# A gated linear recurrence and a feed-forward layer on one core: the last four slabs as one group

## The chip, the cores and the metric

The kernel runs on one core of a Trainium2 chip. The core has five engines that each work through their own list of instructions in order: TensorE (PE, matrix products into PSUM), VectorE (DVE), ScalarE (ACT, functions from tables), GpSimd (POOL) and SyncE (SP, which here only issues transfers). Loads of stationary operands for PE have a row of their own in the profile (PEld). The metric is the device time of one run in microseconds; the kernel before has a median of 265.34 us over 3 runs (265.21 to 265.36). The profiled execution has a span of 263.2 us.

## The reference, cut to what matters

First a recurrence with a complex decay, for 4 batches, 8 heads, 768 steps and 48 features:

```python
mag = np.sqrt(a_re * a_re + a_im * a_im)
scale = np.minimum(mag, 0.999) / (mag + 1e-06)
a_re_n, a_im_n = (a_re * scale, a_im * scale)
for t in range(S):
    new_re = ar * S_re - ai * S_im
    new_im = ar * S_im + ai * S_re
    S_re, S_im = (new_re + kv, new_im)      # kv: outer product of k[t] and v[t]
    y[:, :, t] = np.einsum('bhd,bhde->bhe', q[:, :, t], S_re)
```

Then y, as x of 3072 tokens by 384, goes through a gated feed-forward layer with 1536 inner features:

```python
gate = 1.0 / (1.0 + np.exp(-(x @ w_gate)))
val = x @ w_val
return (gate * val @ w_out).astype(np.float32)
```

## The kernel before, in words

**Slabs.** The 768 steps of a batch are cut into 6 chunks of 128. A chunk of one batch, with all 8 heads, is a *slab*: 128 steps on the partitions by 384 columns. There are 24, numbered chunk by chunk (slab m is batch m % 4 of chunk m // 4). Within a slab the recurrence becomes products of matrices: running sums of the logarithm of the decay and of its angle, q and k scaled by the exponentials and turned by the angles, masked scores of q against k, and a state of 48 by 48 for each head that is carried from chunk to chunk.

**Groups.** Slabs are taken in groups, by SIZES. A group shares the steps on its whole tile of decays (four activations on ScalarE), and, after the recurrence, one feed-forward part: tokens of all its slabs are the columns of its products. With four slabs these are 512 columns, with two 256. Chunk 5, the last, is cut into two groups of two in the kernel before, so there are seven groups.

**Steps.** Every piece of work is a *step* with a short name and a number (slab, or group and block of features). In the order of the data:

- lr, la (L541): loads of a_re and a_im of a slab; sq: squares, on ScalarE (L571) or VectorE (L568); add and min (L577, L584): squared magnitude and its cap.
- lna, lnm (L592, L598), inv (L603), r (L609), atan (L687): logarithms, ratio and angle, for a group.
- cl (L618): running sum of logarithms by a product in fp32; ee (L625, L627): its exponentials; scr, rbe, arr: decay over a chunk, by way of HBM.
- lk, lq, lv (L541): loads of k, q and v; qke (L680): q and k times the exponentials; v16 (L673): v in half precision.
- ct (L701, L704, L723), r16 (L730), nid (L737), hop (L714), cr (L747): running sum of the angle, less whole turns, with the carry from the chunk before; from chunk 2 on the carry is added by a small transfer, hop.
- ab, cs (L758, L769 to L772): cosine and sine; ks, qs (L782): k and q turned, written into a place with six slots.
- transposing of those: by PE (tp, qkT: L820, L821, L827) for the first 13 slabs, by transfers (xk, xq: L803) for the others.
- sc (L839), mst (L847): scores and their mask; u, x16, kv, P (L861, L870, L879, L889): the state; y (L905, L907), y16 (L507): the output of the recurrence; xp, xt (L925, L931): its transposition into xt, the input of the feed-forward part.
- pg and pv (L944): products with w_gate and w_val, for 12 blocks of 128 features, three matmuls each; tanh (L954): the gate, as a tanh; p (L960): (tanh + 1) times the value; po (L980): products with w_out, in three parts of four matmuls for each slab; ot (L507) and st (L998): output and its store.

pg and pv of a group can start once xt of all its slabs is there.

**Order.** Nothing is reordered by a compiler: the order is by hand. TIMES holds a due time for every step, in us; all steps are sorted by it, and each engine gets its instructions in that order. SLOTS says for each buffer of a ring which of its places a tile takes, and WARM how many matmuls on zeros (L1014) are put ahead of a step, into the tile that it will overwrite; they keep PE's clock up while it would wait. When ScalarE needs another set of function tables than the one it holds, a load of a table (L1008) is put in. The due times do not delay anything: an instruction starts when its engine has come to it and its inputs and places are there.

The lines that the change touches are tables alone. SIZES is used in

```python
FIRST = [sum(SIZES[:i]) for i in range(len(SIZES))]
for g, n in enumerate(SIZES):
    m0 = FIRST[g]
    spans = [(i, min(i + PAIR, n)) for i in range(0, n, PAIR)]
nt = n * L
```

and the last slab's output is computed in two halves of 192 columns, so that its first half can be stored while the second is computed.

Of the kernel before, what the change touches and what calls it, by code (L numbers as in the profile page):

```python
# [34 lines left out]
SIZES = [4, 4, 4, 4, 4, 2, 2]  # L35
TIMES = {
    "wg": [
        22.939, 53.604, 46.761],
    "wv": [
        41.489, 57.377, 49.918],  # L40
    "wo": [
        69.384, 65.792, 74.71],
    "lr": [
        0.6, 2.76, 4.68, 1.01, 7.56, 11.4, 21.96, 9.48, 29.035, 36.763,
        34.603, 40.603, 53.574, 65.05, 65.46, 69.488, 91.541, 102.449, 94.661,
        101.489, 129.641, 144.257, 166.92, 169.283],
    "la": [
        1.42, 5.64, 6.6, 3.72, 8.52, 13.32, 21, 14.28, 30.955, 37.723, 44.224,
        38.683, 56.839, 59.355, 66.25, 71.918, 91.951, 100.699, 93.701,
        100.289, 132.576, 136.865, 169.693, 171.783],  # L50
    "sq": [
        5.29, 9.13, 10.09, 7.21, 12.09, 16.953, 26.869, 17.819, 35.119,
        43.141, 51.317, 50.58, 63.932, 71.041, 72.995, 77.727, 96.326, 108.9,
        100.923, 107.686, 141.821, 149.617, 173.785, 176.745],
    "add": [
        6.159, 9.999, 11.044, 8.079, 13.107, 17.97, 27.886, 19.639, 42.886,
        44.046, 52.222, 58.417, 64.837, 72.97, 75.53, 81.618, 99.728, 109.941,
        101.828, 108.978, 146.191, 151.929, 174.69, 177.65],
    "min": [
        10.579, 11.624, 21.17, 29.665, 54.424, 59.948, 80.715, 83.639,  # L60
        111.798, 110.895, 156.229, 185.814],
    "lna": [
        10.958, 34.211, 53.348, 80.235, 115.074, 157.704, 179.252],
    "lnm": [
        12.335, 32.834, 62.547, 84.606, 112.957, 159.31, 186.78],
    "inv": [
        13.712, 36.423, 64.669, 81.743, 117.191, 158.572, 180.12],
    "r": [
        16.087, 15.221, 39.728, 37.968, 67.623, 70.424, 89.8, 94.764, 118.736,
        126.526, 159.477, 181.025],  # L70
    "cl": [
        13.863, 16.67, 20.01, 15.378, 36.319, 37.411, 34.836, 38.883, 64.65,
        68.978, 65.942, 65.296, 86.871, 112.147, 102.388, 106.72, 115.007,
        117.823, 134.023, 131.882, 160.664, 162.183, 192.729, 188.19],
    "ee": [
        15.356, 20.801, 21.541, 20.061, 37.8, 38.54, 35.683, 39.73, 66.046,
        69.825, 68.557, 72.255, 87.718, 114.334, 111.477, 112.217, 116.451,
        118.669, 137.956, 136.74, 161.511, 163.03, 193.576, 189.037],
    "scr": [
        23.34, 22.65, 23.62, 22.37, 44.634, 48.008, 43.366, 48.288, 94.111,  # L80
        85.572, 83.333, 75.858, 96.031, 114.89, 112.033, 112.773, 118.11,
        120.772, 143.977, 139.687, 185.698, 186.798, 194.287, 194.567],
    "rbe": [
        31.915, 61.755, 97.571, 116.08, 149.099, 193.468, 197.428],
    "lk": [
        19.08, 12.36, 23.9, 10.44, 30.542, 22.93, 46.624, 26.99, 86.538,
        74.318, 80.523, 75.448, 103.409, 82.923, 106.289, 108.241, 133.536,
        118.468, 143.567, 127.135, 153.417, 186.388, 158.185, 173.993],
    "lq": [
        20.04, 18.12, 27.942, 16.2, 39.643, 35.803, 47.598, 49.079, 89.103,  # L90
        79.105, 83.883, 76.705, 104.369, 95.621, 107.249, 112.313, 135.905,
        125.596, 148.689, 134.624, 157.07, 193.058, 158.595, 187.724],
    "lv": [
        15.24, 17.16, 35.013, 42.956, 54.152, 67.21, 41.563, 81.87, 92.361,
        85.162, 115.54, 96.581, 105.329, 118.878, 87.987, 130.695, 139.277,
        121.052, 148.279, 126.005, 185.978, 192.648, 170.823, 177.453],
    "v16": [
        20.593, 42.309, 50.738, 49.342, 66.832, 77.757, 59.371, 87.463,
        98.286, 94.188, 124.976, 103.369, 118.084, 149.97, 105.026, 147.632,
        171.078, 133.794, 189.145, 130.048, 191.369, 202.109, 188.569, 183.572],  # L100
    "qke": [
        23.805, 22.502, 32.19, 20.947, 45, 47.581, 55.616, 60.85, 96.525,
        88.039, 91.561, 85.702, 112.701, 115.256, 128.287, 134.657, 148.209,
        164.194, 152.883, 143.564, 162.433, 196.377, 194.498, 198.138],
    "atan": [
        17.39, 41.764, 76.35, 105.833, 131.576, 183.842, 183.105],
    "ct": [
        18.918, 20.953, 26.326, 21.761, 43.292, 45.031, 52.079, 49.241,
        90.692, 86.225, 90.046, 89.232, 122.944, 118.469, 127.422, 128.468,
        141.143, 143.731, 163.053, 166.071, 196.201, 198.47, 197.014, 210.201],  # L110
    "r16": [
        19.765, 22.036, 28.601, 24.671, 44.785, 46.524, 55.711, 53.381,
        92.893, 87.268, 96.023, 92.427, 124.789, 119.316, 128.465, 129.397,
        145.892, 151.604, 163.899, 167.878, 197.481, 201.212, 205.333, 211.683],
    "nid": [
        21.599, 22.636, 29.201, 25.271, 47.8, 47.124, 57.969, 53.981, 95.223,
        89.07, 97.975, 98.138, 125.513, 120.184, 129.686, 131.483, 151.699,
        153.161, 165.483, 170.802, 198.308, 205.144, 206.601, 216.88],
    "cr": [
        25.889, 26.259, 30.065, 26.629, 49.053, 49.423, 59.91, 56.806, 95.586,  # L120
        95.956, 102.136, 104.169, 125.876, 126.246, 130.049, 132.953, 152.062,
        156.041, 176.375, 174.522],
    "cs": [
        23.575, 24.732, 30.542, 29.067, 49.793, 48.055, 58.646, 56.019,
        97.088, 89.752, 102.535, 99.273, 126.617, 120.704, 130.419, 133.335,
        153.726, 154.883, 165.847, 171.166, 198.671, 205.507, 207.141, 217.243],
    "ks": [
        25.137, 27.735, 34.253, 31.008, 53.847, 50.186, 62.767, 63.633,
        100.35, 91.041, 105.9, 103.014, 130.62, 121.993, 133.214, 138.058,
        155.016, 167.012, 173.321, 172.455, 201.678, 209.351, 208.486, 218.665],  # L130
    "qs": [
        26.003, 29.533, 35.985, 36.851, 56.177, 51.783, 69.053, 65.696,
        101.548, 97.554, 107.254, 108.12, 132.348, 123.325, 143.227, 141.296,
        157.143, 168.81, 175.386, 177.145, 203.143, 210.817, 215.684, 219.531],
    "ab": [
        30.542, 29.067, 49.12, 48.055, 58.364, 55.245, 97.088],
    "tp": [
        31.002, 27.003, 30.555, 36.965, 39.976, 38.436, 40.822, 42.338,
        64.204, 60.921, 63.757, 63.31, 71.142, 78.268, 80.861, 67.236,
        111.701, 114.56, 108.014, 104.329, 119.514, 113.24, 112.793, 121.647,  # L140
        155.897, 136.164],
    "qkT": [
        33.056, 33.654, 37.717, 38.315, 42.217, 39.084, 41.618, 43.881,
        65.097, 61.569, 67.856, 64.499, 73.684, 79.317, 83.445, 68.455,
        112.348, 115.942, 110.784, 109.586, 120.713, 114.145, 113.546,
        124.191, 156.545, 146.957],
    "sc": [
        39.752, 39.529, 41.273, 44.584, 47.577, 44.807, 46.784, 48.678,
        69.624, 75.674, 80.638, 79.114, 78.044, 81.308, 86.002, 84.728,
        117.176, 119.961, 115.653, 114.337, 127.199, 125.29, 117.599, 126.326,  # L150
        158.294, 153.974, 148.462, 148.686, 161.31, 159.167, 162.829, 160.041,
        177.84, 180.206, 182.371, 190.582, 191.856, 193.375, 188.836, 189.059,
        217.265, 217.042, 220.489, 220.712, 225.009, 222.435, 227.095, 226.217],
    "mst": [
        40.553, 39.953, 42.815, 45.85, 48.521, 45.251, 47.456, 49.586, 71.295,
        77.073, 81.062, 79.916, 78.711, 81.732, 86.669, 85.212, 117.6,
        121.312, 116.54, 115.343, 127.866, 126.187, 118.666, 126.786, 158.718,
        154.398, 148.887, 151.004, 161.781, 160.25, 163.254, 162.381, 179.769,
        180.968, 186.393, 191.006, 192.589, 193.799, 190.083, 189.483,
        218.066, 217.466, 220.913, 221.978, 227.064, 223.102, 227.663, 229.162],  # L160
    "kv": [
        40.622, 58.131, 77.844, 72.884, 102.188, 82.829, 122.094, 117.399,
        132.528, 134.669, 150.851, 145.025, 166.717, 170.965, 176.345,
        179.358, 201.706, 211.495, 207.411, 220.935],
    "P": [
        41.152, 60.655, 78.245, 74.282, 104.834, 84.746, 122.859, 118.2,
        142.162, 135.07, 153.269, 145.426, 169.676, 178.704, 183.373, 181.567,
        204.867, 213.384, 212.918, 221.512],
    "y": [
        41.739, 46.584, 51.711, 50.533, 78.714, 85.602, 83.678, 88.502,  # L170
# [130 lines left out]
}  # L301
WARM = {
    ('cl', 0): 41,
    ('cl', 2): 8,
    ('cl', 3): 2,
    ('ct', 0): 7,
    ('ct', 2): 16,
# [737 lines left out]
```

## Time and profile before

| | |
|---|---|
| time, median of 3 | 265.34 us |
| span of the profiled execution | 263.2 us |
| PE busy | 240.2 us (91%) |
| VectorE busy | 211.7 us (80%) |
| ScalarE busy | 178.5 us (68%) |
| GpSimd busy | 150.7 us (57%) |
| loads of tables (L1008) | 23, 29.5 us |
| moved by DMA | 38.12 MB, 145 GB/s in the mean |

How to read it: the busy time of PE contains the time in which a matmul drains, so a full row does not say that PE runs at its best pace; the distance between starts of neighbouring matmuls does. In a row of the groups, the numbers behind the bar are the busy time, the mean of one in ns, and the idle time of the engine ahead of them with what ended it. The chain that ended last is followed back from the last instruction, at each step to what released it or to the instruction before it on its engine.

### The profile page before, as it was taken

What the parts mean: (1) busy time and instruction counts of PE and PEld (TensorE: products, weight loads), DVE (VectorE), ACT (ScalarE), POOL (GpSimd) and SP (SyncE); (2) the same over time, 40 slices, a digit from 0 to 9 for tenths busy, and PEclk for the clock granted to TensorE, in tenths of its full rate; (3) what the DMA queues carried; (4) which work ended last, traced back from release to release, by engine and by line L of the source; (5) the groups of instructions that cost most, each with busy time, mean ns of one, the idle gap of its engine ahead of it and who ended that gap; (6) DMA issues with size and microseconds to landing.
All of it is one profiled execution on the core that took longest, in us unless ns stands there. A gap on an engine that the chain in (4) does not pass through costs nothing.

```text
span 263.2 us, 5644 instructions
## 1 busy us (share of the span) xinstructions
PE 240.2 (91%) x2066; PEld 150.2 (57%) x2066; DVE 211.7 (80%) x363; ACT 178.5 (68%) x288; POOL 150.7 (57%) x165
## 2 busy tenths in 40 slices
PE   6076598999999999999999999999999999999995
PEld 6043375454657654547765456654457544679784
DVE  2658998798988979979997889898859689987453
ACT  3799698299999478999469648758974373214240
POOL 3035409969599999679877299833687642010000
PEclk9669989999999999999999999999999999999999
DMA  7999999999999939975699969859964455651011
GB/s 146 218 214 176 192 149 188 205 166 182 139 205 202 181 74 169 176 157 95 121 209 204 151 135 149 194 111 178 221 133 90 66 110 108 73 147 36 8 54 60
DMA packets 174859, 38.12 MB, mean 145 GB/s; under 512 B 167768, under 2 KB 174832, under 8 KB 174832
## 3 DMA queue, kind: packets, MB, share of 16 engines
q1 hardware_dynamic: 170336, 34.20, 68.3%
q0 software_dynamic: 4496, 3.57, 9.7%
q8 instruction: 16, 0.26, 0.4%
q14 instruction: 11, 0.09, 0.1%
HBM read 30.74 MB, written 4.76 MB: 135 GB/s over the span
## 4 chain that ended last, share of the span: by engine, by line
PE 58%; ACT 15%; DMA 8%; DVE 7%; SPq 4%; issue 3%; POOL 3%; ACTq 0%; POOLq 0%
PE o L980 16%; PE v L944 13%; PE g L944 11%; PE cl L618 4%; ACT L1008 4%; DMA a<-in_a_im_dram 3%; PE sc L839 3%; SPq L541 3%; PE ct L723 3%; DMA a<-in_a_re_dram 3%; ACT a L687 2%; POOL qk L680 2%; DMA qk<-in_q_dram 2%; ACT g L954 1%; POOL a L609 1%
## 5 line engine op out<-in xcount | busy, mean ns | idle before, releaser
L954 ACT ACTIVATE g<-g 128x512 f16<-128x512 f32 (+1 forms) x84 | 43.6, 542 | 37.4 <-PE g L944 34.5
L960 DVE SCALAR_TENSOR_TENSOR p<-g,v 128x512 f16<-128x512 f16 (+1 forms) x84 | 49.6, 607 | 20.9 <-ACT g L954 10.1
L944 PE MATMUL v<-xt,wv 128*128 128x512 f16 (+1 forms) x252 | 57.3, 348 | 0.5 <-ACT g L954 0.4
L944 PE MATMUL g<-xt,wg 128*128 128x512 f16 (+1 forms) x252 | 56.9, 348 | 0.5 <-DVE xt L931 0.3
L980 PE MATMUL o<-wo,p 128*128 128x384 f16 (+1 forms) x300 | 54.6, 319 | 0.5 <-ACT g L954 0.5
L577 POOL TENSOR_TENSOR lm<-sq 128x384 f32<-128x384 f32 x20 | 23.2, 1174 | 30.7 <-DVE sq L568 18.9
L680 POOL TENSOR_TENSOR qk<-qk,ee 128x768 f32<-128x768 f32 x20 | 38.2, 1915 | 2.4 <-ACT ee L627 1.6
L847 DVE TENSOR_TENSOR mst<-sc,msk_t 128x512 f16<-128x512 f32 x48 | 32.3, 685 | 4.7 <-PE sc L839 4.6
L944 PEld LDWEIGHTS <-wv 128*128 128x128 f16 x252 | 24.1, 98 | 20.6 <-issue 1.6
L980 PEld LDWEIGHTS <-p 128*128 128x128 f16 x300 | 27.3, 97 | 14.9 <-issue 0.9
L944 PEld LDWEIGHTS <-wg 128*128 128x128 f16 x252 | 23.6, 97 | 20.3 <-issue 2.6
L618 PE MATMUL cl<-lm,wl_t 128*128 128x384 f32 x48 | 22.2, 557 | 9.2 <-ACT lm L598 8.9
L1008 ACT ACT_TABLE_LOAD x23 | 29.5, 1283 | 0.4
L782 DVE TENSOR_TENSOR qst<-qk,cs 128x768 f16<-128x768 f32 x24 | 26.1, 1092 | 0.0
L782 DVE TENSOR_TENSOR kst<-qk,cs 128x768 f16<-128x768 f32 x24 | 24.4, 1029 | 1.4 <-ACT cs L772 0.9
L609 POOL TENSOR_TENSOR a<-a 128x768 f32<-128x768 f32 x10 | 18.1, 1816 | 9.1 <-DMA qk<-in_q_dram 7.8
L571 ACT ACTIVATE sq<-a 128x768 f32<-128x768 f32 x19 | 16.0, 846 | 6.3 <-DMA a<-in_a_im_dram 6.2
L861 POOL TENSOR_TENSOR state<-state,arr 128x384 f32<-128x384 f32 x16 | 13.9, 869 | 11.0 <-DVE state L889 10.7
L827 DVE COPY qkT<-tp 128x1024 f16<-128x1024 f16 x26 | 17.3, 682 | 1.5 <-PE tp L821 1.5
L625 ACT ACTIVATE ee<-cl 128x384 f32<-128x384 f32 x24 | 12.0, 500 | 9.0 <-PE cl L618 6.9
L839 PEld LDWEIGHTS <-qkT 128*128 128x128 f16 x192 | 13.4, 97 | 7.4 <-issue 2.7
L723 PE MATMUL ct<-a,wt_t 128*128 128x384 f32 x40 | 16.9, 507 | 0.6 <-ACT a L687 0.5
(76 smaller groups left out, 428.9 us busy)
## 6 DMA issues: line engine op xcount, KB each, us to landing
a<-in_a_re_dram SPq DMA_DIRECT2D x24, 192.0 KB
a<-in_a_im_dram SPq DMA_DIRECT2D x24, 192.0 KB
qk<-in_k_dram SPq DMA_DIRECT2D x24, 192.0 KB
v<-in_v_dram SPq DMA_DIRECT2D x24, 192.0 KB
qk<-in_q_dram SPq DMA_DIRECT2D x24, 192.0 KB
out_dram<-ot SPq DMA_DIRECT2D x23, 192.0 KB
wg<-in_moe_w_gate_dram POOLq DMA_DIRECT2D x3, 384.0 KB, 6.4
wv<-in_moe_w_val_dram POOLq DMA_DIRECT2D x3, 384.0 KB, 6.4
```

Source lines behind the costliest of these rows:

```text
L577: eng(g).tensor_tensor(out=T[LM][:, s], in0=T[SQ][:, 0], in1=T[SQ][:, 1], op=ALU.add)
L618: nc.tensor.matmul(T[CL][:, :HD], wl_t, T[LM][:, s], start=True, stop=True)
L680: eng(g).tensor_tensor(out=T[QK], in0=T[QK], in1=T[EE], op=ALU.mult)
L723: nc.tensor.matmul(T[CT][:, :HD], wt_t, T[A][:, 1, s], start=True, stop=False, skip_group_check=True)
L782: nc.vector.tensor_tensor(out=T[SL][i].rearrange("p h (r x) -> p h r x", r=2)[:, :, :, 0:D], in0=heads(T[QK][:, i]).unsqueeze(2) .broadcas ...
L839: nc.tensor.matmul(sc[:, i], kt, qt, start=True, stop=True)
L847: nc.vector.tensor_tensor(out=T[MS], in0=T[SC], in1=msk_t.unsqueeze(1).broadcast_to([L, 4, L]), op=ALU.mult)
L944: nc.tensor.matmul(T[ACC][:, :nt], w[:, j, fb * 128:fb * 128 + 128], T[XT][:, j, :nt], start=(j == 0), stop=(j == 2))
L954: nc.scalar.activation(out=T[G16][:, :nt], in_=T[PG][:, :nt], func=FT.Tanh, scale=0.5)
L960: nc.vector.scalar_tensor_tensor(out=T[PT][:, fb, :nt], in0=T[G16][:, :nt], scalar=1.0, op0=ALU.add, in1=T[PV][:, :nt], op1=ALU.mult)
L980: nc.tensor.matmul(T[PO][:, :wd], T[PT][:, fb, s * L:(s + 1) * L], wo16[:, fb, c0:c0 + wd], start=(fb == 0), stop=(fb == NFB - 1))
L1008: nc.scalar.preload_act_table_set(SETS[key[1]])
```

## The change

SIZES gets six groups of four, so that the last four slabs share one feed-forward part of 512 columns, and the steps on a group's tile of decays are done once for the four. It is for fewer and larger instructions on PE, VectorE and ScalarE in the last chunk. As there are fewer steps and their sizes differ, all due times, places in the rings and fillers were computed anew, for all 24 slabs and not for the last four alone. The number of fillers goes from 150 to 211. The code below the tables is unchanged.

```diff
-SIZES = [4, 4, 4, 4, 4, 2, 2]
+SIZES = [4, 4, 4, 4, 4, 4]
 TIMES = {
...
     "lr": [
...
-        129.641, 144.257, 166.92, 169.283],
+        131.683, 136.462, 153.209, 141.067],
     "la": [
...
-        132.576, 136.865, 169.693, 171.783],
+        133.153, 132.373, 157.251, 141.847],
...
     "xt": [
...
-        195.883, 196.5, 197.215, 196.234, 225.6, 225.866, 235.784, 237.901],
+        192.648, 199.472, 198.936, 199.802, 228.285, 229.255, 229.52, 229.786],
     "pg": [
-        55.379, 58.979, 66.588, 57.321, 70.494, 73.731, 67.683, 62.015,
...
+        56.731, 57.378, 74.734, 58.673, 70.649, 68.261, 73.439, 62.637,
...
     "po": [
...
-        239.236, 235.654, 236.958, 238.258, 246.108, 248.069, 249.708,
-        248.719, 249.048, 249.379, 250.358, 250.689, 251.018],
...
+        249.683, 250.993, 246.743, 247.393, 248.703, 251.643, 252.293,
+        252.943, 245.763, 248.043, 248.373, 249.353, 250.333, 250.663],
...
 WARM = {
-    ('cl', 0): 41,
-    ('cl', 2): 8,
-    ('cl', 3): 2,
-    ('ct', 0): 7,
-    ('ct', 2): 16,
-    ('y', 2): 11,
-    ('sc', 3, 1): 9,
+    ('cl', 0): 80,
+    ('cl', 3): 5,
+    ('ct', 0): 10,
+    ('ct', 1): 3,
+    ('ct', 2): 4,
+    ('ct', 3): 6,
+    ('sc', 0, 0): 4,
+    ('y', 0): 3,
+    ('sc', 2, 1): 9,
+    ('y', 2): 2,
+    ('y', 3): 10,
     ('pg', 0, 0): 11,
-    ('cl', 4): 15,
-    ('cl', 6): 30,
+    ('cl', 4): 10,
+    ('cl', 6): 37,
+    ('ct', 4): 5,
+    ('ct', 5): 10,
+    ('ct', 6): 2,
 }
```

## The prediction, made before the changed kernel was run

> **What bounds the kernel now.** I read the page first, for the busy shares and the forty slices.
>
> ```profile
> PE 240.2 (91%) x2066; PEld 150.2 (57%) x2066; DVE 211.7 (80%) x363; ACT 178.5 (68%) x288; POOL 150.7 (57%) x165
> PE   6076598999999999999999999999999999999995
> PEclk9669989999999999999999999999999999999999
> ```
>
> TensorE is full from the ninth slice (about 58 us) to the end, and its clock is low only in the head. Since a busy PE row counts drain time, I checked this against the cadence, in the chain that ended last:
>
> ```profile
> 223.43 0.65 PE v L944 x3
> 224.07 1.30 PE o L980 x8
> 240.22 0.33 PE g L944 x3
> 256.74 3.29 PE o L980 x32
> 260.06 0.36 DVE ot L507
> ```
>
> Three 512-column matmuls take 0.65 us (216 ns each), three 256-column ones 0.33 us (109 ns), four of 384 columns 0.65 us (162 ns). From neighbouring rows, fp32 products over 384 columns come at 325 ns a record, 128-column ones at 55.5 ns and 48-column ones at about 25 ns. Multiplying by the counts by form gives 217.0 us of useful PE work; 21.1 us of it is ordered ahead of the first gate product, 195.9 us behind it. From that product to the last one the trace has 260.06 - 58.65 = 201.4 us. So behind 58.65 us all PE waiting together is only 5.5 us, and the kernel is: **head (58.65) + PE work (195.9) + waits (5.5) + tail (3.1) = 263.2**.
>
> ```profile
> 57.57 0.78 PE L1014 MATMUL g<-zero 128*128 128x128 f16 x11
> 58.65 0.81 PE L944 MATMUL g<-xt,wg 128*128 128x512 f16 x3 [0.29 <-DVE xt L931]
> ```
>
> This timeline of PE shows the head's end: filler matmuls, then the first gate product, released by VectorE's xt.
>
> Each step has its due time in TIMES, so trace minus table is how far the chip lags the plan. The first pg is due at 55.379 and starts at 58.65: lag 3.27. It grows to 3.8 at 91 us, 4.6 at 96, 5.6 at 115, 6.65 at 143, 6.97 at 188, 8.2 at 197, and then stays at 8.3 to 8.5 up to the last product. The table thus orders the work and also spaces PE's work rightly; what it misses is 3.3 us in the head and 5.2 us of small waits between 60 and 200 us. The last of these, 1.25 us, shows in the chain:
>
> ```profile
> 176.08 0.57 SPq L541
> ...
> 176.70 4.67 DMA a<-in_a_im_dram
> ...
> 182.85 1.07 ACT g L954 x2
> ...
> 188.97 1.28 ACT L1008
> ...
> 190.27 0.61 ACT g L954
> ...
> 190.91 2.11 PE o L980 x12
> ```
>
> A load of a_im for slab 22 was due at 169.7, was issued at 176.70, and held back ScalarE's square; the tanh queued behind it was late, and with it p and the output products.
>
> **What the Trainium skill says.** "TensorE: Matmul & The Clock Gate", section "Wait — 56ns, not 53.3ns?", gives a fixed 2.5 ns for each matmul above its columns. This trace agrees: 2 x 109.2 - 216 is 2 to 3 ns, so halving the width is nearly free on PE. The same page, "What's actually happening", has the clock gate halve the clock after an idle window of some 3.4 us; PEclk at 0.58 between 10 and 20 us agrees. "ScalarE: Activation LUTs", section "What ACT_TABLE_LOAD costs", has 1283 ns for each load; the 23 loads here measure 1283 ns.
>
> **The change part by part.** The rows by form that price it:
>
> ```profile
> L944 PE MATMUL v<-xt,wv 128*128 128x256 f16 x72 | 11.0, 272 | 0.0
> L960 DVE SCALAR_TENSOR_TENSOR p<-g,v 128x512 f16<-128x512 f16 x60 | 40.0, 682 | 13.9 <-ACT g L954 6.5 <-PE v L944 6.1 <-ACT sq L571 0.9
> L960 DVE SCALAR_TENSOR_TENSOR p<-g,v 128x256 f16<-128x256 f16 x24 | 9.6, 419 | 7.0 <-ACT g L954 3.6 <-PE v L944 3.0
> L954 ACT ACTIVATE g<-g 128x512 f16<-128x512 f32 x60 | 34.7, 606 | 16.4 <-PE g L944 15.0 <-DVE p L960 1.1
> L954 ACT ACTIVATE g<-g 128x256 f16<-128x256 f32 x24 | 8.9, 384 | 21.0 <-PE g L944 19.6 <-DVE p L960 1.4
> ```
>
> *Merging on PE.* 144 matmuls of 109.2 ns (15.7 us) become 72 of 216 ns (15.55): 0.2 us less on the bound engine. The output products are per slab and stay.
>
> *Merging on VectorE and ScalarE.* p: 24 x 419 = 10.06 us becomes 12 x 682 = 8.18, so 1.9 us less; tanh: 24 x 384 becomes 12 x 606, also 1.9 us less; four steps on slabs (two Ln, Exp, Arctan) go from two of 844 ns to one of about 1488, 0.8 us less. Table loads: reading the new TIMES in order gives 20 in place of 23, 3.8 us less. All this lies beside PE, so I cost it at nothing by itself; it can only shorten the 5.2 us of waits.
>
> *The tail.* Before, the last feed-forward part had 256 tokens and ran while the other half was still being prepared. Now all four slabs must be transposed into xt before the last part begins. The new table puts its first pg at 230.223, and the last xt at 229.786 in place of 237.901, so the recurrence has to finish 8 us sooner. What hides this is other PE work placed ahead of 230: the group before it is ordered up to there. PE gaps planned there are small: from first pg to last po the new table spans 252.943 + 0.65 - 56.731 = 196.9 us for 195.9 us of work, about 0.9 us of planned gaps against none before. After my 0.2 us rounding: **+0.7**.
>
> *The head.* First pg due at 56.731 in place of 55.379, with 20.93 us of useful work ahead of it in place of 21.13. So 1.35 + 0.2 = **+1.55 us**. I see no reason that the head's lag of 3.27 should differ: the same loads come at about the same places (45 of slabs due by 50 us in both tables), and the fillers rise from 150 to 211, each in a planned gap (37 ahead of the fifth cl, in a gap of 3.99 us; at the halved clock's 111 ns that is 4.1).
>
> *The end.* The last output was the second 192 columns of slab 23 (0.36 us of VectorE, 96 KB store). Now slab 22's full 384 columns come last: 0.56 us and 192 KB. 0.2 on VectorE; the extra 96 KB at the span's mean of 145 GB/s would be 0.7, at the 200 GB/s of the busiest slices 0.5, and much of this overlaps issuing; bounds 0 to 0.7, taken as 0.2. **+0.4**.
>
> *Waits.* The late loads of slabs 22 and 23 were due at 166.9 to 171.8 for squares due at 173.8 and 176.7. The new table asks for them at 153.2 and 157.3 for a square at 180.5 (slab 22) and at 141.1 and 141.8 for one at 154.6 (slab 23): 23 and 13 us of room in place of 4 to 5. I expect the 1.25 us of lag that they made to go: **-1.2**. The waits between 60 and 188 us (some 3.7 us) I keep: the order there is as crowded, with 79 loads due by 80 us in place of 77 (a weight load, twice the size, counted as two).
>
> Sum: 1.55 + 0.7 + 0.4 - 1.2 = +1.45, so 265.34 + 1.45 = **266.8 us**.
>
> **The rivals.**
>
> *Waits stay as they were.* If the 1.2 us moves elsewhere rather than goes, 265.34 + 2.65 = 268.0. For it: every freshly made order meets its own late load, SyncE's issues lagging the table by up to 9 us in this trace. Against it: the loads near the end have much room now.
>
> *The last handoff stalls.* VectorE has 28.2 us of work due between 200 and 230 us, and the chain from Arctan (due 192.9) to the last xt runs through one set of four slabs with only 4.0 us from the last transposing load to its score products (4.9 before). If that chain lags PE by two or three us, PE stands before the last part: 268.0 + 2.5, about 270.5. Against it: with 27.5 us due on VectorE in the same stretch before, PE did not wait at all after 205 us.
>
> *Faster, the other side.* The relief of ScalarE (5.7 us with three loads fewer) and VectorE takes most of the mid-kernel waits, which do pass through ScalarE (tanh lags to 5.7 us at 113 us while p lags 4.7). If 4 of the 5.2 us go: 265.34 + 2.65 - 4.0 = 264.0. Against it: the mid waits start at loads and at GpSimd, which the merging doesn't touch before 150 us.
>
> **How the numbers follow.** Forecast (266.8) 0.42, waits stay (268.0) 0.25, last handoff (270.5) 0.11, faster (264.0) 0.22. The head's lag of 3.27 alone may turn out 1 us either way, which spreads each of them. The range leaves out most of the handoff case and the better half of the faster one: 264.4 to 269.4. From the same cases: faster by over 0.2% (below 264.8) 0.19, within 0.2% 0.13, slower 0.68.
>
> **What would show it.** Right: first gate product of full width at 59.5 to 60.5 us, about 196 us of PE work behind it with no long stretch of another engine, the last product ending at 261.5 to 262.5; 20 or 21 table loads; no wait at slabs 22 and 23. Wrong: first gate product by 58.7 us, or its lag not growing between 60 and 200 us (then the faster case); a gap of over 1 us on PE, released by xt, ahead of the last gate products (then the handoff); large idle rows of PE waiting on tanh or p.

## The result and the profile after

The changed kernel takes 267.07 us against 265.27 us (265.01 to 265.36) for the kernel before beside it: ratio 1.0069, 95% interval 1.0049 to 1.0088. It is slower by about 1.8 us, close to the forecast of 266.8. Runs over 1.5% above the fastest of the same kernel (three of the changed kernel's eleven, at 272.2 to 272.3 us, one of e_end and two of e_port) count in the medians but not in the ratios. First the page of the changed kernel: busy times, PE's row of the slices, and two of the groups.

```profile
PE 242.8 (91%) x2055; PEld 147.9 (56%) x2055; DVE 209.9 (79%) x351; ACT 172.9 (65%) x269; POOL 152.0 (57%) x164
PE   8186488887999999999999999999999999999994
...
L958 ACT ACTIVATE g<-g 128x512 f16<-128x512 f32 x72 | 41.7, 598 | 42.6 <-PE g L948 30.3
L964 DVE SCALAR_TENSOR_TENSOR p<-g,v 128x512 f16<-128x512 f16 x72 | 48.0, 683 | 15.6 <-PE v L948 8.4
```

The merging did what it was for: 72 tanh and 72 p in place of 84 each, all of 512 columns, 5.6 us less on ScalarE and 1.8 us less on VectorE. PE's row is full from the eleventh slice on; the slice before it, from 59.7 to 66.3 us, holds the pause that is shown below.

I split each profiled execution at the first gate product of full width and at the end of the last product. The splits sum to the span, so this table says where each kernel's time lies, in us:

| kernel | to the first gate product | from it to the last product's end | from there to the end | span |
|---|---|---|---|---|
| before | 58.65 | 201.37 | 3.15 | 263.17 |
| changed | 60.88 | 200.75 | 3.74 | 265.37 |
| difference | +2.23 | -0.62 | +0.59 | +2.20 |

The profiled execution of the kernel before took 264.89 us, 0.4 less than its median of 265.27; that of the changed kernel took its median. This is why the spans differ by 2.20 us and the medians by 1.80.

So the whole loss is in the head and in the last store; the long stretch of PE between them, where the merging acts, is a little shorter. Trace minus table, the measure of the prediction, divides it further:

| at (us of the trace) | 60 | 70 | 120 | 186 | 200 | 250 |
|---|---|---|---|---|---|---|
| lag before | 3.26 | 3.50 | 5.70 | 6.93 | 8.22 | 8.34 |
| lag changed | 4.14 | 5.55 | 6.11 | 7.54 | 7.63 | 7.85 |

Three things are to be seen. The changed kernel enters with 0.9 us more lag. It loses 1.4 us at once between 60 and 70, where the kernel before loses 0.2. And the step of 1.3 us between 186 and 200 is gone. The list of PE's waits behind the head (columns: us in total, times, longest) has little in it; these are the longest:

```profile
PE ct L741 <- DVE r L734: 1.3, 1, 1.3
PE y L909 <- POOL x L874: 0.4, 1, 0.4
```

The longest of them in the timelines of PE, VectorE and GpSimd (columns: start, duration):

```profile
60.88 1.46 PE L948 MATMUL g<-xt,wg 128*128 128x512 f16 x6
...
65.56 0.32 PE L741 MATMUL ct<-r,nid_t 128*128 128x384 f16 x1 [1.28 <-DVE r L734]
```

```profile
61.61 0.95 DVE L786 TENSOR_TENSOR kst<-qk,cs 128x768 f16<-128x768 f32 x1
62.48 2.56 DVE L786 TENSOR_TENSOR qst<-qk,cs 128x768 f16<-128x768 f32 x1
64.97 0.54 DVE L734 TENSOR_SCALAR r<-ct 128x384 f16<-128x384 f32 x1
```

```profile
62.22 2.01 POOL L613 TENSOR_TENSOR a<-a 128x768 f32<-128x768 f32 x1 [2.08 <-ACT a L607]
```

PE stands 1.28 us for r16, which stood on VectorE behind a qs that took 2.56 us where its twin took 0.95. A GpSimd product had begun 0.26 us before that qs and ended at 64.23; the qs ended at 65.04, 0.81 us later. "SBUF — State Buffer" of the Trainium skill, section "SBUF: two separate sides", says why: a port pair that VectorE, with two inputs in SBUF, and GpSimd take as an exclusive lock for a whole instruction, so that the second one waits. This trace agrees: the held qs needs nearly its normal time after the GpSimd operation, and no more. The kernel before has this too, at 59.44 us:

```profile
59.44 2.02 DVE L782 TENSOR_TENSOR qst<-qk,cs 128x768 f16<-128x768 f32 x1
```

Beside it GpSimd ran qke from 58.83 to 60.64, and this qs ended at 61.46, again 0.82 us after. There PE waited for nothing behind it. Over whole traces the holds are alike: of the products that turn q and k, 10 take over 0.15 us longer than 0.95 us before, 5.1 us in excess together, and 9 after, 4.8 us. What differs is who stood behind one of them.

The end of the changed kernel, in VectorE's timeline, is the 384-column output that the prediction named:

```profile
261.67 0.56 DVE L511 TENSOR_SCALAR ot<-o 128x384 f32<-128x384 f32 x1 [1.12 <-PE o L984]
```

### The profile page after: what moved, and what is told of

It reads as the page before. It is cut to its first block, busy times and chain, and to the rows that moved or that the text cites. A ratio compares the mean times of both kernels' runs of the same rounds, so it can differ in the third digit from the quotient of the medians.

```text
span 265.4 us, 5540 instructions
## 1 busy us (share of the span) xinstructions
PE 242.8 (91%) x2055; PEld 147.9 (56%) x2055; DVE 209.9 (79%) x351; ACT 172.9 (65%) x269; POOL 152.0 (57%) x164
## 4 chain that ended last, share of the span: by engine, by line
PE 49%; issue 1%; POOL 1%; ACT 0%; DVE 0%; POOLq 0%
PE o L984 13%; PE v L948 12%; PE g L948 12%; PE ct L727 3%; PE sc L843 2%; PE cl L622 2%; PE y L909 1%; PE y L911 1%; PE xp L929 1%; PE kv L883 1%; PE ct L741 1%; POOL x L874 0%; PE tp L824 0%; PE tp L825 0%; POOL state L865 0%
## 5 line engine op out<-in xcount | busy, mean ns | idle before, releaser
L958 ACT ACTIVATE g<-g 128x512 f16<-128x512 f32 x72 | 41.7, 598 | 42.6 <-PE g L948 30.3
L964 DVE SCALAR_TENSOR_TENSOR p<-g,v 128x512 f16<-128x512 f16 x72 | 48.0, 683 | 15.6 <-PE v L948 8.4
L948 PE MATMUL v<-xt,wv 128*128 128x512 f16 x216 | 55.3, 379 | 0.0
L948 PE MATMUL g<-xt,wg 128*128 128x512 f16 x216 | 54.8, 379 | 0.0
L948 PEld LDWEIGHTS <-wg 128*128 128x128 f16 x216 | 20.4, 98 | 22.7 <-issue 0.9
L948 PEld LDWEIGHTS <-wv 128*128 128x128 f16 x216 | 20.4, 98 | 22.4 <-issue 0.5
L677 POOL TENSOR_SCALAR v<-v 128x384 f16<-128x384 f32 x24 | 16.1, 670 | 7.4 <-DMA v<-in_v_dram 5.5
L1018 PEld LDWEIGHTS <-zero 128*128 128x128 f16 x211 | 16.2, 114 | 6.1 <-issue 4.6
L773 ACT ACTIVATE cs<-ct 128x384 f32<-128x384 f32 x17 | 8.4, 492 | 17.0 <-PE ct L741 16.8
L865 POOL TENSOR_TENSOR state<-state,arr 128x384 f32<-128x384 f32 x16 | 15.3, 961 | 7.1 <-DVE state L893 6.7
## 6 DMA issues: line engine op xcount, KB each, us to landing
a<-in_a_re_dram SPq DMA_DIRECT2D x24, 192.0 KB
a<-in_a_im_dram SPq DMA_DIRECT2D x24, 192.0 KB
qk<-in_k_dram SPq DMA_DIRECT2D x24, 192.0 KB
qk<-in_q_dram SPq DMA_DIRECT2D x24, 192.0 KB
v<-in_v_dram SPq DMA_DIRECT2D x24, 192.0 KB
out_dram<-ot SPq DMA_DIRECT2D x23, 192.0 KB
```

What stands on the lines that cost most here:

```text
L948: nc.tensor.matmul(T[ACC][:, :nt], w[:, j, fb * 128:fb * 128 + 128], T[XT][:, j, :nt], start=(j == 0), stop=(j == 2))
L958: nc.scalar.activation(out=T[G16][:, :nt], in_=T[PG][:, :nt], func=FT.Tanh, scale=0.5)
L964: nc.vector.scalar_tensor_tensor(out=T[PT][:, fb, :nt], in0=T[G16][:, :nt], scalar=1.0, op0=ALU.add, in1=T[PV][:, :nt], op1=ALU.mult)
```

## The experiments

My theory after the result: the loss belongs to the order that was made anew (head, hold, end), and the group of four costs nothing in itself. The first rival: the group of four itself costs time, since all four slabs must be ready before its last part begins. The second, on the 1.3 us at 186 to 200: late loads made it, as I had predicted, or the table loads did. Ratios are to the kernel before, run on the same chip.

**The old head under the changed kernel (e_head).** All steps due before the first pg at their places of before, with its fillers; all later ones 1.352 us earlier; three steps at the seam have due times of their own.

```diff
 "lr": [
-        0.6, 6.6, 4.68, 3.72, 7.56, 14.28, 10.44, 21, 24.272, 43.543, 34.765,
+        0.6, 2.76, 4.68, 1.01, 7.56, 11.4, 21.96, 9.48, 29.035, 36.763,
...
 "lnm": [
-        12.335, 34.763, 56.018, 85.111, 114.137, 184.828],
+        12.335, 32.834, 54.666, 83.759, 112.785, 183.476],
...
 WARM = {
-    ('cl', 0): 80,
+    ('cl', 0): 41,
```

> The changed kernel, with the order and the fillers of the head (all steps due ahead of the first gate product) taken from the kernel before; the rest of the changed kernel's order stands, moved up by 1.35 us. Theory 1 (the loss lies in the head as it was ordered anew): the first gate product starts near 58.7 us in place of 60.9, and the time falls by about 2.2 us, to 264.9 us, below the kernel before. Theory 2 (the loss comes from the last group of four, which cannot start until four slabs are done): the first gate product comes earlier, but the time stays near 267 us, with PE waiting later instead. Theory 3 (a different head only shifts waits into the first feed-forward part): the gain is under 1 us, 266 to 267 us.

Measured: 271.64 us, 1.0263 (1.0235 to 1.0292). The first gate product came at 65.63 us, the stretch behind it was 200.3. PE's waits between 40 and 75 us, and GpSimd's timeline:

```profile
PE y L909 <- POOL v L675: 4.5, 2, 3.4
```

```profile
53.53 2.55 POOL L682 TENSOR_TENSOR qk<-qk,ee 128x768 f32<-128x768 f32 x1 [2.46 <-DMA qk<-in_q_dram]
```

My splice was bad: where the halves met, qke of slab 6 stood on GpSimd ahead of two v16 that PE needed, and it waited for its load of q. So this kernel doesn't test the theory. It does show how the head multiplies a misplaced step: a wait of 2.46 us on GpSimd held PE for 4.5, its clock was at half from 54 to 68 us, and the first gate product came 6.98 us (65.63 - 58.65) later than in the kernel before. Only 0.5 us of it was won back against the changed kernel's stretch.

**The same, mended (e_head2).** Four steps at the seam moved: qke of slab 6, add of slab 11, min of slabs 10 and 11, and lnm of the third group (the la of slab 12 goes along by 0.03 us). The lines with a minus are those of e_head.

```diff
 "add": [
-        44.046, 52.222, 50.5805, 67.101, 71.917, 81.258, 70.959, 98.792,
+        44.046, 52.222, 51.6, 67.101, 71.917, 81.258, 70.959, 98.792, 103.086,
...
 "min": [
-        10.579, 11.624, 21.17, 29.665, 54.424, 52.796, 80.355, 82.792,
+        10.579, 11.624, 21.17, 29.665, 54.424, 53, 80.355, 82.792, 107.348,
...
 "lnm": [
-        12.335, 32.834, 54.666, 83.759, 112.785, 183.476],
+        12.335, 32.834, 55.3, 83.759, 112.785, 183.476],
...
 "qke": [
-        23.805, 22.502, 32.19, 20.947, 45, 47.581, 48.06, 61.928, 87.679,
+        23.805, 22.502, 32.19, 20.947, 45, 47.581, 55.616, 61.928, 87.679,
```

> The changed kernel with the head of the kernel before, as in the first such run, but with qk of slab 6 scaled after v of slabs 2 and 3 on GpSimd (that order had made y wait for v), and the sums and caps of slabs 10 and 11 where they stand in the changed kernel. If the loss lies in the newly ordered head: first gate product near 58.7 us and a time of 264 to 265.5 us, level with the kernel before. If the later parts of the new order cost the 2 us: first gate product near 58.7 us, time 266.5 us or more.

Measured: 265.97 us against 264.49, 1.0045 (1.0028 to 1.0061); the first gate product came at 60.21, the stretch took 200.5. Less than a third of what I expected of the head came, 0.67 us of 2.2. The timelines of PE and of VectorE say what held the rest:

```profile
60.21 2.72 PE L946 MATMUL g<-xt,wg 128*128 128x512 f16 x6 [0.81 <-DVE xt L933]
```

```profile
55.59 1.45 DVE L784 TENSOR_TENSOR qst<-qk,cs 128x768 f16<-128x768 f32 x1
```

This product on VectorE, and the next at 58.16 us with 1.46, were held again (0.5 us each); GpSimd ran adds and minima beside them. xt came 0.81 us late. And then six gate matmuls took 2.72 us where the changed kernel takes 1.46: PE's clock was at half from 60.0 to 63.4 us. The prediction quotes "TensorE: Matmul & The Clock Gate" of the Trainium skill, section "What's actually happening", for a clock that is halved after an idle window of some 3.4 us. No such window is in this trace: PE's longest pause in the 14 us before is the one of 0.81 us, and what halved the clock stays open.

**More room for the late loads (e_room).** The kernel before, with the decays of its last two slabs in the unused half of the tile of the two before, so that their loads can go 8 to 10.5 us earlier.

```diff
 "lr": [
-        101.489, 129.641, 144.257, 166.92, 169.283],
+        101.489, 129.641, 144.257, 158.9, 160.3],
 "la": [
-        100.289, 132.576, 136.865, 169.693, 171.783],
+        100.289, 132.576, 136.865, 159.3, 161.3],
...
-        A, LM = t_a2(g), t_lm(g)
+        o = 2 if g == 6 else 0
+        A, LM = A if o else t_a2(g), t_lm(g)
...
-                def e(T, A=A, s=s, b=lo + s, c=c, i=i, src=src):
+                def e(T, A=A, s=s + o, b=lo + s, c=c, i=i, src=src):
```

> The kernel before with its seven groups, where the seventh group keeps its decays in the unused half of the sixth group's tile, so that the loads of a_re and a_im for slabs 22 and 23 need not wait for a place and are ordered 8 to 10 us sooner. Nothing else is moved. If the late loads made the last 1.25 us of lag (the prediction's step on waits), the lag between 180 and 200 us goes and the time falls by about 1.2 us, to 264.1 us. If those waits have another cause (tables and the crowded list of ScalarE), the squares come sooner but the tanh and the output products do not, and the time stays within 0.4 us of 265.3 us.

Measured: 265.23 us, 1.0020 (1.0008 to 1.0032): nothing gained. But the trace has a new wait in it. The stores of two outputs, which SyncE issued at 168.62 us in the kernel before, now stand behind the four early loads and go out at 171.88; an output on VectorE waits for a place, and PE's lag grows by 0.8 us, from 7.1 to 7.9, between 175 and 179 us. VectorE's timeline:

```profile
174.74 0.56 DVE L520 TENSOR_SCALAR ot<-o 128x384 f32<-128x384 f32 x1 [1.12 <-DMA out_dram<-ot]
```

ScalarE's timeline of this kernel:

```profile
181.71 0.83 ACT L586 ACTIVATE sq<-a 128x768 f32<-128x768 f32 x1
...
185.80 0.60 ACT L969 ACTIVATE g<-g 128x512 f16<-128x512 f32 x1
186.42 1.28 ACT L1023 ACT_TABLE_LOAD   x1
187.71 0.84 ACT L607 ACTIVATE a<-a 128x768 f32<-128x768 f32 x1
188.59 0.84 ACT L618 ACTIVATE a<-a 128x768 f32<-128x768 f32 x1
189.45 1.28 ACT L1023 ACT_TABLE_LOAD   x1
190.74 1.09 ACT L969 ACTIVATE g<-g 128x512 f16<-128x512 f32 x2
```

The square waits no longer, and yet the lag at 200 us is 8.7, more than in the kernel before; from 186 us on it grows by 0.8, there by 1.3. PE's one wait for a tanh in this stretch, ahead of the output products of slab 14, is 0.33 us; in the kernel before it is 0.53. The tanh itself came no earlier (190.74 against 190.27): PE was late by then, and two tanh behind the square, at 183.15 and 183.80, start 0.02 us after their gate products end. So this kernel doesn't say what the late load was worth. The trace of the kernel before gives a bound, in the timelines of ScalarE and of PE:

```profile
181.46 0.85 ACT L571 ACTIVATE sq<-a 128x768 f32<-128x768 f32 x1 [0.63 <-DMA a<-in_a_im_dram]
...
182.84 1.08 ACT L954 ACTIVATE g<-g 128x512 f16<-128x512 f32 x2
...
190.27 1.09 ACT L954 ACTIVATE g<-g 128x512 f16<-128x512 f32 x2
```

```profile
181.33 1.46 PE L944 MATMUL g<-xt,wg 128*128 128x512 f16 x6
```

From the square, which is 0.63 us late, to the tanh at 190.27, ScalarE's list runs with pauses of no more than 0.03 us. With the load in time, the second of the two tanh at 182.84, which starts at 183.33, would still have had to wait for the end of its gate product at 182.79 (181.33 + 1.46), so it could have come 0.54 us sooner at most. By this estimate the late load may have had the 0.53 us of PE's wait, but not the whole 1.3 us. In the same list, ScalarE's rows show a second candidate: between two tanh 4.34 us go by with two loads of tables (1.28 each) and two slab activations (0.84 each).

**The tables away from those tanh (e_tables).** The kernel before, with the Ln, the exponential (inv) and the Arctan of the last slabs moved behind the tanh of the group before. The steps that hang on them go along (r, ct, hop).

```diff
 "lna": [
-        10.958, 34.211, 53.348, 80.235, 115.074, 157.704, 179.252],
+        10.958, 34.211, 53.348, 80.235, 115.074, 157.704, 184.7],
 "inv": [
-        13.712, 36.423, 64.669, 81.743, 117.191, 158.572, 180.12],
+        13.712, 36.423, 64.669, 81.743, 117.191, 158.572, 185],
...
 "atan": [
-        17.39, 41.764, 76.35, 105.833, 131.576, 183.842, 183.105],
+        17.39, 41.764, 76.35, 105.833, 131.576, 184.62, 193.8],
```

> The kernel before, with the logarithm and the exponential of its seventh group, the arctangent of the sixth, and the steps that hang on them, moved behind the last tanh of the fourth group, so that no table is loaded in the midst of those tanh (two loads and two activations stood between them from 185.9 to 190.3 us). The number of loads stays the same. If these loads made the last 1.25 us of lag, the lag between 185 and 195 us stays near 7 us and the time falls by about 1.2 us against the kernel before, a ratio near 0.995. If the wait moves to the recurrence of slabs 22 and 23, which now starts later, the ratio is 1.0 or above.

Measured: 266.89 us, 1.0087 (1.0069 to 1.0104), slower. No output product waits for a tanh between 175 and 206 us any more; but the lag, 6.89 at 186 us, is 8.98 at 200 and 10.51 at 230. PE's longest waits behind the head:

```profile
PE cl L629 <- ACT lm L609: 1.3, 1, 1.3
PE g L955 <- ACT g L965: 0.7, 1, 0.7
```

The wait went where the tables went, while a square still stood 0.88 us for its late load. So the wait needed the tables and activations amid the tanh; a late load alone doesn't make it. But a sum of logarithms (cl) now waits for its Ln, later in the same chain: in the kernel before, moving these steps alone saves nothing. In the changed kernel the list of PE's waits is empty between 175 and 206 us. In its timeline of ScalarE the next load of tables comes after the last of these tanh, and one Ln serves four slabs:

```profile
190.60 0.60 ACT L958 ACTIVATE g<-g 128x512 f16<-128x512 f32 x1 [0.73 <-PE g L948]
191.21 1.28 ACT L1012 ACT_TABLE_LOAD   x1
192.50 1.48 ACT L602 ACTIVATE lm<-lm 128x1536 f32<-128x1536 f32 x1
```

**The new order without the merging (e_split).** The changed kernel with its last group again two of two; both groups keep their decays in one tile, slabs 22 and 23 change places in the loads and squares, and the two feed-forward parts run one after the other.

```diff
-SIZES = [4, 4, 4, 4, 4, 4]
+SIZES = [4, 4, 4, 4, 4, 2, 2]
 "pg": [
...
-        205.788, 202.189, 200.247, 214.119, 205.14, 230.87, 236.05, 230.223,
+        205.788, 202.189, 200.247, 214.119, 205.14, 230.547, 233.137, 230.223,
+        234.108, 234.756, 231.518, 235.079, 237.022, 232.489, 231.841,
...
```

> The changed kernel with its order, its head and its fillers, but with the last group cut into two of two again: 144 gate and value matmuls of 256 columns in place of 72 of 512, two sets of the four activations on decays (both in one tile), 24 tanh and 24 p of 256 columns. Theory 1 (merging is nearly free on PE and worth little beside it): 267.2 to 267.6 us. Rival (merging's relief of ScalarE and VectorE shortened the waits by over 1 us): above 268.2 us. A second rival (the group of four holds the last part back): below 266.6 us, since half of the last part can start sooner, though its place in the order is kept.

Measured: 269.25 us, 1.0156 (1.0132 to 1.0180), about 2 us above the changed kernel. The lag is that of the changed kernel up to the last part (7.84) and grows to 9.51 in it, 1.6 us of the 2.2 by which the spans differ; the rest is in the end, 4.28 us in place of 3.74, where one output waits 2.4 us for a store. PE's timeline in the last part:

```profile
250.41 0.82 PE L962 MATMUL v<-xt,wv 128*128 128x256 f16 x6
251.06 0.49 PE L962 MATMUL g<-xt,wg 128*128 128x256 f16 x3
251.48 0.49 PE L962 MATMUL v<-xt,wv 128*128 128x256 f16 x3
251.90 0.81 PE L962 MATMUL g<-xt,wg 128*128 128x256 f16 x6
```

With 256 columns PE is through a block of three matmuls in 0.33 us, yet two of these start 0.42 us ahead of the next. From 238 to 255 us, 16 matmuls start over 0.02 us late, 1.5 us together, and 15 of them start within 0.05 us of the end of a tanh or of a p. A block needs one of four places in PSUM, which a tanh or a p frees, and these can't follow when nothing else lies between. The kernel before has narrow blocks too, but between other work, and its lag stays at 8.34 to 8.51 there. So in an order in which the last part runs by itself, four slabs together are worth some 1.6 us of PE's time. That is the rival that I had named for this run, relief worth over 1 us, and not my theory that it is worth little. This kernel also has 20 loads of tables: fewer loads come from the order, not from the merging, against what I had said.

**The merging in the old order (e_merge).** The kernel before with the last two groups as one; seven steps of slabs 20 and 21 move behind the activations that all four now share, and the last part starts after the last xt.

```diff
-SIZES = [4, 4, 4, 4, 4, 2, 2]
+SIZES = [4, 4, 4, 4, 4, 4]
 "lnm": [
-        12.335, 32.834, 62.547, 84.606, 112.957, 159.31, 186.78],
+        12.335, 32.834, 62.547, 84.606, 112.957, 186.78],
...
 "pg": [
...
-        208.259, 205.306, 202.554, 201.906, 201.059, 226.44, 229.029, 233.031,
+        208.259, 205.306, 202.554, 201.906, 201.059, 239.556, 244.736,
...
```

> The kernel before with its last two groups merged and next to nothing else remade: all due times stay, apart from seven steps of slabs 20 and 21 that have to follow the shared activations, and the last feed-forward part, which comes as one after slab 23's xt. This takes 7.9 us of gate and value products and 2.6 us of output products away from the stretch where the recurrence of slabs 22 and 23 ends. If the late group must be filled with other work (the prediction's step on the tail), PE stands there and the time is 270 to 275 us. If the order matters little, about 265.2 us.

Measured: 273.64 us, 1.0336 (1.0304 to 1.0369). The stretch behind the first gate product took 209.5 us. PE's longest waits, and its busy time in the window that lost most (columns: window, length, then busy us and instructions of PE):

```profile
PE o L987 <- ACT g L961: 1.8, 1, 1.8
PE cl L625 <- ACT lm L605: 1.6, 1, 1.6
```

```profile
190.00:200.00 10.00, 6.60 (x33) 3.29 (x30) 2.90 (x5) 7.15 (x8) 7.87 (x8) 0.83 0.48 92
```

Of the ten microseconds from 190 us, 3.4 are at half the clock (192.0 to 195.4). The first rival has a part of the truth: the sums of logarithms of slabs 20 and 21, due at 160.7 and 162.2 us before, now wait for the decays of the last two slabs and come at 186.8, the last part waits for all four, and in the old order, with no more moved than this, that costs 8 us of the stretch. A new order can avoid most of it.

**Single holds in the changed kernel (e_swap, e_port).** In e_swap r16 of slab 6 goes ahead of the held qs; in e_port the qs goes later.

```diff
 "r16": [
-        19.765, 22.326, 24.268, 27.462, 46.122, 47.972, 59.182, 53.572,
+        19.765, 22.326, 24.268, 27.462, 46.122, 47.972, 57.6, 53.572, 86.014,
```

> The changed kernel with one due time altered: the rounding r16 of slab 6 goes ahead of the last qs of slab 4 on VectorE. In the changed kernel that qs took 2.56 us in place of 0.95, held while GpSimd multiplied two operands (62.22 to 64.23 us), and the matmul nid of slab 6, queued on PE behind it, stood for 1.28 us. If this hold is what lengthens the waits behind the first gate product, nid no longer waits and the time falls by 1.0 to 1.3 us against the changed kernel, to a ratio of 1.002 to 1.003. If VectorE itself is the bound there, the same wait comes back at the next product that needs it, and the ratio stays near 1.007.

```diff
 "qs": [
-        25.73, 27.928, 37.022, 33.825, 58.316, 56.584, 75.437, 68.385, 97.254,
+        25.73, 27.928, 37.022, 33.825, 60.5, 56.584, 75.437, 68.385, 97.254,
```

> The changed kernel with one due time altered: qs of slab 4, a product of two operands on VectorE, goes behind r16 of slab 6, P of slab 1 and ab of slab 6, at 60.5 in place of 58.316, so that it no longer starts while GpSimd multiplies two operands. No step is taken away. If the hold of 1.6 us that it met there is what made the wait behind the first gate product, it takes about 0.95 us, neither nid of slab 6 nor kv of slab 2 waits on PE, and the time falls by 1.0 to 1.3 us against the changed kernel. If PE's place in the plan is set by something else, the wait comes back within 10 us and the time stays within 0.4 us.

Measured: e_swap 266.85 us, 1.0080 (1.0063 to 1.0096); e_port 269.33 (six runs from 266.39 to 270.50), 1.0126 (1.0085 to 1.0167). PE's longest wait behind the head in e_port:

```profile
PE g L954 <- DVE p L970: 2.6, 1, 2.6
```

Neither gained in the mean; e_port's runs lie far apart, its fastest 0.5 us below the fastest of the changed kernel, and the trace is of a run of 270.06. In e_swap the r16 was early, and the copy of the state, also behind the held qs, made PE wait 1.1 us in its place. In e_port the qs met the next GpSimd product; the timelines of VectorE and of GpSimd:

```profile
64.93 2.58 DVE L792 TENSOR_TENSOR qst<-qk,cs 128x768 f16<-128x768 f32 x1
```

```profile
64.89 1.81 POOL L619 TENSOR_TENSOR a<-a 128x768 f32<-128x768 f32 x1
```

It began 0.04 us too late, ended 0.81 us after the GpSimd product as the others did, and this time p was behind it; after PE's wait of 2.59 us the clock was at half from 70.6 to 74.0 us. That the hold costs about 1.3 us stands on the changed kernel's own trace; neither of these two edits took it out.

**The end (e_end).** The changed kernel with slab 23's halves last.

```diff
 "po": [
...
-        227.203, 220.086, 224.406, 226.553, 220.736, 222.26, 223.356, 246.093,
-        249.683, 250.993, 246.743, 247.393, 248.703, 251.643, 252.293,
-        252.943, 245.763, 248.043, 248.373, 249.353, 250.333, 250.663],
+        227.203, 220.086, 224.406, 226.553, 220.736, 222.26, 223.356, 246.4,
+        250, 250.65, 246.743, 247.393, 248.703, 245.763, 248.043, 249.353,
+        251.3, 251.63, 251.96, 252.29, 252.62, 252.95],
```

> The changed kernel with the output products of slab 23, in their two halves, put behind those of slab 22, so that the last output is 192 columns and its store 96 KB, as in the kernel before. By the prediction's step on the end this is worth 0.4 us: the stretch from the last product to the end falls from 3.7 to about 3.2 us. If the end is set by something else (how the stores queue on SyncE), no change.

Measured: 266.60 us, 1.0071 (1.0054 to 1.0088). VectorE's last step has 192 columns and takes 0.36 us, and the span ends 3.25 us after the last product in place of 3.74. The half microsecond is in the trace, but the ratio doesn't tell it from the changed kernel's.

**The changed kernel again (c_after).** A second measurement of the same kernel, beside e_port and e_best.

> The changed kernel again, unaltered, so that the two beside it are compared with it on one chip: ratio near 1.007 to the kernel before.

Measured: 267.16 us, 1.0086 (1.0065 to 1.0106). Together with the first, the loss is 0.7 to 0.9%.

**Head and end together (e_best, e_best2).** e_best is e_head2 with the inv of the third group ahead of its lnm, a load of w_gate 1.6 us earlier, more fillers ahead of the first pg, and slab 23 last; e_best2 also orders the outputs slab by slab.

```diff
 "wg": [
-        22.939, 53.604, 46.761],
+        22.939, 52, 46.761],
...
 "inv": [
-        13.712, 36.423, 56.043, 81.567, 117.115, 186.361],
+        13.712, 36.423, 55.2, 81.567, 117.115, 186.361],
...
 WARM = {
...
-    ('pg', 0, 0): 11,
+    ('pg', 0, 0): 24,
```

> The changed kernel with the head of the kernel before, as in the second such run, with three additions: 24 fillers in place of 11 ahead of the first gate product (PE's clock had dropped to half from 60.0 to 63.4 us), the exponential of the third group ahead of its logarithm so that the first tanh need not wait for the caps, and the halves of slab 23 as the last output. If the head, the clock behind it and the end make the whole loss, the parts sum to 1.3 to 1.7 us for the clock and 0.5 for the end, and the ratio to the kernel before comes to 0.997 to 1.0. If the merged group loses time for itself, the ratio stays above 1.003.

```diff
 "po": [
...
-        222.004, 245.048, 248.648, 249.298, 245.391, 246.041, 247.351,
-        244.411, 246.691, 248.001, 249.948, 250.278, 250.608, 250.938,
+        222.004, 248.298, 248.948, 249.598, 244.411, 245.048, 246.348,
+        245.698, 246.998, 247.648, 250.248, 250.578, 250.908, 251.238,
...
```

> The run before it (head of the kernel before, 24 fillers, slab 23 last) with the output products taken slab by slab (21, 22, 20, 23) so that the outputs come about 1.5 to 2 us apart. There, three outputs had stood behind a store of 3.00 us because two places hold the outputs, and 4.2 us passed from the last product to the end. If that is so, this stretch falls to about 3.3 us, the time falls by about 0.9 us, and the ratio to the kernel before is 0.997 to 0.999: level or just ahead, with the group of four. If not, the ratio stays at 1.001.

Measured: e_best 265.09 us, 1.0014 (1.0000 to 1.0028), first gate product at 59.60, end 4.2 us, since the last outputs stood behind a store of 3.00 us with two places for ot; e_best2 264.53 us against 264.64, 0.9995 (0.9982 to 1.0007), first gate product at 59.82 and end 3.28. With its group of four, e_best2 can't be told from the kernel before. The loss was thus the new order's own: against the changed kernel's trace, that of e_best2 gains 1.06 us in the head, 0.46 in the end and 0.34 between. The changes were made together, so their shares are read from traces and not from runs of their own. Behind its first gate product no r16 holds PE: the lag goes from 4.44 at the first gate product to 4.27 at 70 us, where the changed kernel loses 1.4. The two also warn of reading a table of splits too finely: they differ only in the last outputs, yet their stretches differ by 1.2 us (profiled executions of 264.82 and 265.30 us, one faster and one slower than its median), half of it a load of wv that came 0.6 us late at 75 us in the one profiled execution and not in the other.

## Why the prediction was right, point by point

*The head, +1.55: right in kind, 0.7 us short.* The first pg was ordered 1.35 us later and came 2.23 us later. The term that failed is "I see no reason that the head's lag of 3.27 should differ": it was 4.15. It grew in small steps, 2.3 us at 48.8, 3.15 at 53.7, 3.8 at 56.2, with PE waits of 0.25 to 0.56 us on VectorE and ScalarE among them, not at one load. e_head2 and e_best2 moved it by about 0.7 and 1.1 us, so the head's order is shown as the place, though no single wait in it is. In the second measurement (c_after) the loss is 2.3 us, 0.8 above the forecast, about what this term lacks.

*Merging on PE, VectorE and ScalarE, nothing but 0.2 us: right* for the old kernel's shape: relief of ScalarE by 5.6 us bought nothing on the path by itself, and e_merge, which also has the merging, is slower. One thing I missed: where the last part stands alone, as it does in the new order, the wide form is worth some 1.6 us of PE's time (e_split), which I had put at nothing. The smaller number of table loads I put under the merging; e_split has it without the merging.

*The tail, +0.7: right.* No gate product waits for xt behind the head in the changed kernel, and the lag grows only 0.2 us from 200 to 250. From first pg to the end of the last po the new table has 0.9 us more than the old, 0.7 with the shorter PE work. The longer table was in the forecast as such; that the order had to be made anew for this is e_merge's 8 us.

*The end, +0.4: right*, +0.59 measured, of which e_end took back 0.49.

*Waits, -1.2: right in size by luck, too much given to one cause.* The lag grew by 3.7 us from the first pg to 250 us in place of 5.1, so 1.4 us less; the 1.3 us between 186 and 200 became 0.1. But I had given the whole step to the late loads. The load that I named held ScalarE for 0.63 us and can have cost 0.54 at most; e_tables kept the late loads, took the tables away and lost the wait for the tanh, to meet another. e_room, meant to test the loads alone, brought a wait of its own. In the changed kernel the loads come earlier and the tables behind these tanh, which I had not looked at; which of the two took the wait away stays open. I had followed the chain of waits back to the DMA, past a table load that stood in it, in the lines I quoted. Of that step of 1.3 us, 0.7 is at the tanh, 0.3 at 189 us, where a gate product waited for a p, and 0.3 at the sum of logarithms at 196 us; what makes the last two stays open. The 3.7 us of waits up to 186 us which I kept were 3.4, with one new hold of 1.3 us in it that I hadn't seen, and as much less elsewhere; that these cancel is luck too.

*The rivals.* "Waits stay as they were" took the right measure of a fresh order: it did make new waits, in the head and at 62 us, but the old one went, so 268.0 was not reached. "The last handoff stalls" is refuted by the waits. "Faster" fails because the waits up to 186 us stayed, 3.4 us against 3.7.

Summed, the forecast of +1.45 was composed of +1.55, +0.7, +0.4 and -1.2; the profiles gave +2.23, -0.62 for tail, work and waits together (forecast -0.5), and +0.59. What stays open: which steps of the head make its 0.7 us, and whether a still better head exists for the group of four.

## What to carry to other kernels

In this kernel, a merging that saves instructions beside the bound engine was worth only the waits that it removed on that engine, and the order that had to be made anew for it cost or gained more. Judge a new order by three numbers: when the bound engine's steady stretch begins, how far the trace lags the plan along it, and what stands last. And when a wait has a DMA at the far end of its chain, price the other instructions in the chain too, and ask how much sooner they could have run, before naming the DMA as the cause.

## What was not expected of the hardware

A VectorE product with two inputs in SBUF was held while a GpSimd operation ran, and then took 0.81 or 0.82 us from that one's end, in three traces: 0.95 us became 2.02, 2.56 and 2.58 us. The GpSimd operation need not have two inputs: in e_head2 a product that took 1.46 us ended 0.80 us after a minimum of one input. It works both ways: in e_port GpSimd's product, which takes 1.81 us, took 2.52 when VectorE was in its way. With nine or ten such holds, 5 us in all, what they cost PE depends on what stands behind them on VectorE: 1.28 us for one hold in the changed kernel, nothing for that at 59.44 us in the kernel before.

A pause of PE of 0.81 us at the head's end was followed by six matmuls at half the clock, 2.72 us in place of 1.46 (e_head2); in e_best2, with 24 fillers in place of 11 ahead of the same matmuls and a pause of 0.21 us, they took 1.46 us. The length of a single pause doesn't decide it: the changed kernel's pause of 1.28 us at 65.56 had no half clock behind it.
